# Sparse attention into a Mish MLP on one core: x of batches 4 to 7 transposed by VectorE, strided heads staggered by one block, w_out's second half released by landed v

## The chip, the core and the metric

The kernel runs on one core of a Trainium2 chip. The core has five engines with a queue of instructions each: TensorE (matrix products, PE), VectorE (DVE), ScalarE (ACT), GpSimd (POOL) and SyncE (SP), which here only issues transfers. Each engine works through its own queue in order, and engines wait for one another by semaphores. Data lies in HBM, is moved by DMA into SBUF, and TensorE writes its results to PSUM. The metric is the device time of one execution in microseconds, the median of several runs.

## What is computed

Two layers of work, one behind the other:

```python
# q, k, v: 8 batches x 8 heads x 576 positions x 64
scores = q @ k.T / sqrt(64)
# heads 0 to 3, "local":   0 <= i - j < 32
# heads 4 to 7, "strided": i >= j and i % 32 == j % 32
attn = softmax(where(mask, scores, -1e9)) @ v
x = attn.transpose(0, 2, 1, 3).reshape(4608, 512)
h = x @ w_in                      # 512 -> 2048
g = h * tanh(softplus(h))         # Mish
out = g @ w_out                   # 2048 -> 512
```

## The kernel before

**Blocks.** The MLP works on nine blocks of 512 tokens, t = 0 to 8. In block t the first layer (`mlp1`, L410) makes eight groups of 16 matmuls of 512 columns; a group fills one of three PSUM buffers of two banks (`acc`, L87), which ScalarE empties with Mish. The second layer (`mlp2`, L435) then runs 16 groups of four matmuls into two of these buffers, and ScalarE copies the output out twice per block. The buffers' names rotate from block to block (x, y, z in the loop at L585).

**Attention.** Batch 0 comes ahead of the loop. The attention of batch t + 1 is spread over the second layer of block t: `attn_steps` (L358) gives a list of 16 lists, and the loop at L614 runs list i behind the i-th second-layer group. The steps are Q (`qk`: scores of a part of the units into an `acc` buffer, then ScalarE's exponential into P_s or P_l), M (`mask`, L284: VectorE multiplies by the mask), V (`pv`: four matmuls with v into one of two small PSUM buffers, `tile_t`, then VectorE's reciprocal and product, L311 and L312, into x_s or x_l) and X (`xt`: TensorE transposes x into a `tile_t` buffer and ScalarE copies it to xT, which the first layer of the next block reads). A column of ones beside v gives the sum for the softmax. xT is a ring for four batches. A batch has 16 strided units (in parts of 6, 6 and 4) and 12 local units (5, 5 and 2).

**Inputs.** GpSimd issues the loads of strided q and k, which cast on the way (`load_qk_str`), and of the weights. SP issues the loads of local q and k and of all v as f32 (`load_qk_loc`, `load_v`); GpSimd casts them one block later (`cast_qk_loc`, `cast_v`, L144). From batch 2 on, q and k are turned by transposing transfers on SP (`transpose_by_dma`, L163), put at list 9 of the block before the one that uses them. At the end of block t, SP gets the loads for batch t + 3. SP works in order, so a waiting output or transpose holds back the loads behind it.

**Release of w_out.** The loads of w_in and the first half of w_out are issued ahead of the loop. In `cast_v1` (L574, called in block 0) VectorE casts the strided v of batch 1, and GpSimd then copies four elements of the cast into `held`. That copy only makes GpSimd wait: behind it in its queue stand the loads of w_out's second half, of ks and qs of batch 2, and the casts of batches 1 and 2. In block 0 the second layer goes through w_out a quarter at a time over all four token tiles (`fc_major`), so the third quarter is first needed at its ninth group.

**Order.** All queues are in the order in which the program is written (`manual_schedule`); no scheduler moves anything.

Of the kernel before, what the change touches and what calls it, by code (L numbers as in the profile page):

```python
# [38 lines left out]
def kernel(ctx, tc, q, k, v, moe_w_in, moe_w_out, out):  # L39
# [28 lines left out]
    vs = [const.tile([128, 4, CS, D + 1], BF16, name=f"vs{i}") for i in range(2)]  # L68
    qTl = const.tile([128, 2, S], BF16, name="qTl")
    kTl = const.tile([128, 2, 32 + S], BF16, name="kTl")  # L70
    qTs = const.tile([128, 16 * SU], BF16, name="qTs")
    kTs = const.tile([128, 16 * SU + 48], BF16, name="kTs")
    P_s = [const.tile([PN, 2, n * PN + 56], BF16, name=f"Ps{i}") for i, n in enumerate((6, 6, 4))]
    P_l = [const.tile([128, 2, n * WQ + 32], BF16, name=f"Pl{i}") for i, n in enumerate((5, 5, 2))]
    gate = const.tile([1, 256], BF16, name="gate")
    held = const.tile([1, 4], BF16, name="held")
    x_l = const.tile([128, NW, 256], BF16, name="x_l")
    x_s = const.tile([128, CS, 256], BF16, name="x_s")

    g_pool = ctx.enter_context(tc.tile_pool(name="gp", bufs=2))  # L80
    small = ctx.enter_context(tc.tile_pool(name="small", bufs=4))
# [5 lines left out]
    def acc(i, name):  # L87

        return ps_a.tile([128, 2, 512], F32, tag=f"acc{i}", name=name)

    def tile_t(name):
        return ps_t.tile([128, 512], F32, tag="pt", name=name)


    def load_qk_str(b):
        for dst, src in ((ks, k), (qs, q)):
# [27 lines left out]
    def load_v(b):  # L124
        load_v_str(b)
        load_v_loc(b)
# [33 lines left out]
            "p (t i e d) -> p t i e d", t=2, i=NW, e=2  # L160
        )

    def transpose_by_dma(b):  # L163
        for src, dst in ((ks, kTs), (qs, qTs)):
            nc.sync.dma_start_transpose(
                dst[:, 0:16 * SU].rearrange("c (u n) -> c u n", u=16),
                src[b % 2][0:SU].rearrange("p h x -> p (h x)"),
            )
        for hp in range(2):
            for src, dst in ((kl, kTl[:, hp, 32:32 + S]), (ql, qTl[:, hp, :])):  # L170
                nc.sync.dma_start_transpose(
                    dst.rearrange("c (i n) -> c i n", i=NW),
                    by_tile(src[b % 2])[:, hp].rearrange("p i e d -> p (i e d)"),
                )
# [19 lines left out]
    def t_step(b, kind, which, hp, eng=None):  # L194

        eng = eng or nc.vector
        tr = tile_t("tr")[:].bitcast(BF16)
        if kind == "s":
            src = (qs if which == "q" else ks)[b % 2]
            for u in range(8):  # L200
                h, jj = 2 * hp + u // 4, u % 4
                nc.tensor.transpose(
                    tr[:, PN * u:PN * u + PN],
                    src[0:PN, h, 128 * jj:128 * jj + 128],
                    ident[0:PN, 0:PN],
                )
            dst = (qTs if which == "q" else kTs)[:, 8 * SU * hp:8 * SU * hp + 8 * SU]
# [41 lines left out]
        "s": [S_UNITS[0:6], S_UNITS[6:12], S_UNITS[12:16]],  # L249
        "l": [L_UNITS[0:5], L_UNITS[5:10], L_UNITS[10:12]],  # L250
    }
    AT = {kd: {u: (i, n) for i, p in enumerate(PARTS[kd]) for n, u in enumerate(p)} for kd in "sl"}

    class Attn:
        def __init__(self, b):
# [1 line left out]

        def qk(self, parts, i_acc):

            ps, o = acc(i_acc, "ps"), 0  # L260
            todo = []
            for kind, i in parts:
                w = WQ if kind == "l" else PN
                o0 = o
                for x, y in PARTS[kind][i]:
                    for e in range(2):
                        r = slice(64 * e, 64 * e + 64)
                        if kind == "l":
                            lhsT, rhs = kTl[r, y, WQ * x:WQ * x + 128], qTl[r, y, WQ * x:WQ * x + WQ]
                        else:  # L270
                            c0 = SU * (4 * y + x)
                            lhsT, rhs = kTs[r, c0:c0 + 128], qTs[r, c0:c0 + PN]
                        nc.tensor.matmul(ps[:, e, o:o + w], lhsT=lhsT, rhs=rhs, start=True, stop=True)  # L273
                    o += w
                todo.append((kind, i, o0, o - o0))
            for kind, i, o0, nw in todo:
                n, pt = (128, P_l[i]) if kind == "l" else (PN, P_s[i])
                nc.scalar.activation(pt[0:n, :, 0:nw], ps[0:n, :, o0:o0 + nw], AF.Exp, scale=scale)  # L278

        def mask(self, kind, i, meng):  # L280
            nu = len(PARTS[kind][i])
# [8 lines left out]
        def pv_mm(self, kind, i, po):  # L290
            for h in range(4):
                if kind == "l":
                    n, rhs = 128, vl[self.b % 2][:, i, h, :]
                    part, u = AT["l"][i, h // 2]
                    pt, c0 = P_l[part][:, h % 2], WQ * u
                else:
                    n, rhs = PN, vs[self.b % 2][0:PN, h, i, :]
                    part, u = AT["s"][i // 2, h]
                    pt, c0 = P_s[part][:, i % 2], PN * u
                nc.tensor.matmul(  # L300
                    po[:, h, :], lhsT=pt[0:n, c0:c0 + 128], rhs=rhs,
                    start=True, stop=True,
                )
# [51 lines left out]
                    tr[:, 0:576].rearrange("p (j n) -> p n j", j=CS),  # L355
                )

    def attn_steps(b, x, y):  # L358

        a = Attn(b)  # L360
        Q = lambda i_acc, *parts: (lambda: a.qk(parts, i_acc))
# [4 lines left out]
        if x == y:  # L366
# [13 lines left out]
                [V("l", 3), V("l", 4)],  # L380
                [X("l", 0), X("l", 1)], [],
            ]
        return [
            [],
            [Q(x, s0), Q(y, s1), M(*s0), M(*s1)],
            [],
# [10 lines left out]
            [V("l", 4), X("l", 0)],  # L397
            [X("l", 1)], [],
        ]


    def segs(t):
# [7 lines left out]
    def mlp1(t, accs):  # L410
        gT = g_pool.tile([128, 16, 512], BF16, tag="gT", name="gT")

        held = {}

        def group(g, ccs=(2, 3, 0, 1)):
            if g not in held:
                held[g] = acc(accs[g % 3], "psh")
            ps = held[g]
            for u in range(2):
                fc = 2 * g + u  # L420
                for a, n, o in segs(t):
# [12 lines left out]

    def mlp2(t, gT, accs, fc_major=False):  # L435
        po = {}
# [43 lines left out]
    with tc.manual_schedule():  # L480
# [92 lines left out]

        def cast_v1():  # L574
            cast(Dv, vs[1][0:PN, :, :, 0:D], vs32[0:PN])
            Po.tensor_copy(held[:], vs[1][0:1, 3, 0, 0:4])
            load_w_out(2, 4)
            load_qk_str(2)
            cast_v_loc(1, Po)
            load_v(2)  # L580
            cast_qk_loc(2, Po, Po)
            load_qk_str(3)
            cast_v(2, Po, Po)

        for t in range(NBLK):  # L585
            x, y, z = accs
            if t > 0:
                gT, g1 = mlp1(t, accs)
            ts, at = [], []
# [62 lines left out]
```

## Time and profile before

| what | value |
|---|---|
| median of 4 runs | 325.6 us (324.75 to 328.02) |
| the profiled execution | 326.07 us, its span 324.3 us |
| TensorE matmul busy | 303.4 us (94%) |
| ScalarE busy | 173.5 us (53%) |
| VectorE busy | 105.2 us (32%) |
| GpSimd busy | 90.3 us (28%) |
| first-layer matmuls (L423) | 640, 128.3 us |
| second-layer matmuls (L443) | 512, 127.9 us |
| mean transfer rate | 139 GB/s, 45.15 MB |

Busy time of a matmul overlaps its neighbour's, so the profile's start-to-start distances say more than durations: an undisturbed group of four 512-column matmuls takes 0.86 us. The 40 slices are 8.1 us each. A line of the time line gives the start, the duration, the engine, the line of the code, what is done, how many, and in brackets the engine's idle time before it and what ended it. In the chain of waits each line is a start, a length and what held the end back there. A window's line gives its length, the busy time and instructions of the five engines in turn, the granted TensorE clock, the share of the transfer engines and the rate.

### The profile page before, as it was taken

The numbers are of one execution on the slowest core, as the hardware profiler recorded it, in microseconds if no ns is written. First come the engines' busy times: TensorE is split into PE (matmuls) and PEld (weight loads), VectorE is DVE, ScalarE is ACT, GpSimd is POOL, SyncE is SP. The second block draws the span as 40 slices with busy tenths as digits, with TensorE's granted clock in tenths as the row PEclk, the third lists the DMA queues.
The fourth block names the chain that finished last, engine by engine and source line by source line (L and its number), as shares of the span: only waits on it lengthen the run. The fifth ranks groups of instructions, "written<-read, shape, count | busy, mean of one in ns | idle before, by whom it ended". The sixth has DMA issues, their size and how long they took to land.

```text
span 324.3 us, 5880 instructions
## 1 busy us (share of the span) xinstructions
PE 303.4 (94%) x2488; PEld 160.4 (49%) x2488; DVE 105.2 (32%) x289; ACT 173.5 (53%) x196; POOL 90.3 (28%) x100
## 2 busy tenths in 40 slices
PE   0678996999999998999999999999999999999995
PEld 0563453544455444544568655445544554444444
DVE  8671165510381039202830183018301830000000
ACT  2583652285737572666466745674567457315601
POOL 9288019420273048004700480047000000000000
PEclk9999999799999999999999999999999999999999
DMA  7999999997999996999399939993820101011012
GB/s 185 210 212 205 217 186 221 187 158 190 196 194 150 222 179 139 139 222 166 90 162 190 197 91 167 197 185 94 136 85 0 64 3 67 0 65 65 2 55 74
DMA packets 96985, 45.15 MB, mean 139 GB/s; under 512 B 79040, under 2 KB 89600, under 8 KB 96960
## 3 DMA queue, kind: packets, MB, share of 16 engines
q1 hardware_dynamic: 85520, 35.66, 59.3%
q0 software_dynamic: 11152, 8.92, 18.6%
q8 instruction: 19, 0.31, 0.4%
q10 hardware_dynamic: 288, 0.21, 0.2%
q14 instruction: 6, 0.05, 0.1%
HBM read 36.78 MB, written 9.44 MB: 143 GB/s over the span
## 4 chain that ended last, share of the span: by engine, by line
PE 68%; DVE 12%; DMA 8%; SPq 6%; POOL 2%; ACT 1%; issue 1%; POOLq 0%
PE psh L423 32%; PE pso L443 23%; DMA vl<-in_v_dram 6%; PE pso L470 4%; PE po L300 4%; DMA w_out<-in_moe_w_out_dram 3%; POOL vl L144 2%; SPq L115 2%; DVE x_l L312 2%; SPq L109 2%; PE ps L273 2%; DVE x_s L312 2%; PE trx L339 2%; DVE Pl L284 1%; DVE ks L144 1%
## 5 line engine op out<-in xcount | busy, mean ns | idle before, releaser
L443 PE MATMUL pso<-w_out,gT 128*128 128x512 bf16 x512 | 127.9, 382 | 2.2 <-DMA w_out<-in_moe_w_out_dram 2.2
L423 PE MATMUL psh<-xT,w_in 128*128 128x512 bf16 (+1 forms) x640 | 128.3, 362 | 0.0
L428 ACT ACTIVATE gT<-psh 128x1024 bf16<-128x1024 f32 x72 | 73.6, 1024 | 45.0 <-PE psh L423 44.4
L423 PEld LDWEIGHTS <-w_in 128*128 128x128 bf16 x640 | 63.0, 99 | 62.9 <-issue 2.7
L443 PEld LDWEIGHTS <-gT 128*128 128x128 bf16 x512 | 43.9, 98 | 41.9 <-issue 3.4
L284 DVE TENSOR_TENSOR Ps<-Ps,consts_sb 72x864 bf16<-72x864 bf16 (+1 forms) x24 | 16.9, 706 | 114.9 <-ACT Ps L278 114.9
L142 ACT COPY xT<-trx 128x576 bf16<-128x576 bf16 x32 | 20.1, 638 | 39.6 <-PE trx L349 30.7
L144 POOL CAST kl<-kl 96x768 bf16<-96x768 f32 (+1 forms) x13 | 11.9, 938 | 81.0 <-DMA kl<-in_k_dram 80.9
L144 POOL CAST vl<-vl 128x768 bf16<-128x768 f32 (+2 forms) x30 | 26.0, 867 | 11.7 <-DMA vl<-in_v_dram 9.8
L450 ACT COPY osb<-pso 128x1024 f32<-128x1024 f32 x16 | 16.2, 1012 | 22.6 <-PE pso L443 13.5
L278 ACT ACTIVATE Ps<-ps 72x864 bf16<-72x864 f32 (+1 forms) x24 | 18.5, 804 | 13.3 <-PE ps L273 13.2
L311 DVE RECIPROCAL rden<-po 72x4 f32<-72x4 f32 (+1 forms) x100 | 17.4, 174 | 21.1 <-PE po L300 21.0
L312 DVE TENSOR_TENSOR x_s<-po,rden 72x256 bf16<-72x256 f32 x56 | 23.5, 420 | 1.9
L278 ACT ACTIVATE Pl<-ps 128x960 bf16<-128x960 f32 (+1 forms) x24 | 18.7, 806 | 6.4 <-PE ps L273 5.7
L300 PEld LDWEIGHTS <-Ps 72*128 72x128 bf16 x256 | 14.1, 102 | 14.3 <-DVE Ps L284 2.8
L300 PE MATMUL po<-vs,Ps 72*128 72x65 bf16 x256 | 17.9, 202 | 2.0 <-DVE vs L144 0.9
L312 DVE TENSOR_TENSOR x_l<-po,rden 96x256 bf16<-96x256 f32 x44 | 18.5, 420 | 1.5
L144 DVE COPY osb<-pso 128x512 f32<-128x512 f32 (+1 forms) x2 | 1.1, 558 | 54.5 <-PE pso L470 54.5
L300 PE MATMUL po<-vl,Pl 128*128 128x65 bf16 x192 | 13.1, 202 | 2.6 <-DVE rden L311 1.0
L144 POOL CAST vs<-vs 72x2048 bf16<-72x2048 f32 x6 | 12.0, 2008 | 9.2 <-DMA vs<-in_v_dram 6.1
L144 POOL CAST ql<-ql 96x768 bf16<-96x768 f32 (+1 forms) x13 | 11.9, 939 | 9.2 <-DMA ql<-in_q_dram 9.2
L470 PE MATMUL pso<-w_out,gT 128*128 128x512 bf16 (+1 forms) x80 | 14.0, 336 | 0.0
(65 smaller groups left out, 177.8 us busy)
## 6 DMA issues: line engine op xcount, KB each, us to landing
out_dram<-osb SPq DMA_DIRECT2D x16, 512.0 KB, 4.0
vs<-in_v_dram SPq DMA_DIRECT2D x8, 576.0 KB
vl<-in_v_dram SPq DMA_DIRECT2D x8, 576.0 KB, 9.3
kl<-in_k_dram SPq DMA_DIRECT2D x7, 576.0 KB, 18.0
ql<-in_q_dram SPq DMA_DIRECT2D x7, 576.0 KB, 9.9
w_out<-in_moe_w_out_dram POOLq DMA_DIRECT2D x4, 512.0 KB, 15.2
ks<-in_k_dram POOLq DMA_DIRECT2D x7, 288.0 KB, 8.8
qs<-in_q_dram POOLq DMA_DIRECT2D x7, 288.0 KB, 9.2
```

Source lines behind the costliest of these rows:

```text
L142: nc.scalar.copy(out_, in_)
L144: eng.tensor_copy(out_, in_)
L278: nc.scalar.activation(pt[0:n, :, 0:nw], ps[0:n, :, o0:o0 + nw], AF.Exp, scale=scale)
L284: meng.tensor_tensor(out=pm, in0=pm, in1=mk[0:n, :].unsqueeze(1).unsqueeze(1).to_broadcast([n, 2, nu, w]), op=ALU.mult,)
L300: nc.tensor.matmul(po[:, h, :], lhsT=pt[0:n, c0:c0 + 128], rhs=rhs, start=True, stop=True,)
L311: nc.vector.reciprocal(rden[0:m, :], po[0:m, :, D])
L312: nc.vector.tensor_tensor(out=dst.rearrange("p (h d) -> p h d", h=4), in0=po[0:m, :, 0:D], in1=rden[0:m, :].unsqueeze(2).to_broadcast([m, ...
L423: nc.tensor.matmul(ps[:, u, o:o + n], lhsT=w_in[:, cc, fc * 128:(fc + 1) * 128], rhs=xT[:, cc, a:a + n], start=(cc == 2), stop=(cc == 1),)
L428: nc.scalar.activation(gT[:, 2 * g:2 * g + 2, :], ps[:], AF.Mish)
L443: nc.tensor.matmul(p[:, ot % 2, :], lhsT=gT[:, fc, 128 * ot:128 * ot + 128], rhs=w_out[:, fc, :], start=(fc == 0), stop=(fc == 15),)
L450: nc.scalar.copy(osb[:], p[:])
L470: nc.tensor.matmul(p, lhsT=gT[:, fc, 128 * ot:128 * ot + 128], rhs=w_out[:, fc, c0:c1], start=(fc == 0), stop=(fc == 15),)
```

## The change

Four things are changed together.

1. **x of batches 4 to 7** goes to xT without TensorE. VectorE transposes blocks of 32x32: 12 instructions of 384 elements per partition for the local heads, straight into xT (`xt_loc`), and 12 of 512 for the strided heads into a new buffer xs_t (`xt_str`), which two ScalarE copies bring to xT (`xt_str_copy`). Rows 64 to 95 of x_s are cleared once by GpSimd in block 3, since a transpose reads 96 rows.
2. **The strided heads are staggered by one block from batch 4 on.** Their scores are made one block earlier, in parts of 7, 7 and 2 units (kind "n"), beside the local heads of the batch before; batch 4's at the end of block 2. Their products with v and their transposes run between the first-layer groups of the next block (`str_steps`). The local heads keep their block (`loc_steps`). qTs and kTs are doubled, and loads and transposing transfers of strided q and k move one block ahead: GpSimd issues those of batches 4 and 5 in block 1, and SP issues batch 4's transposes in block 1 between the loads of q, k and of v.
3. **The first layer** of blocks 1 to 8 does the strided half (chunks 2 and 3) of its first three groups before their local half.
4. **`held`** copies from the f32 v, so that GpSimd waits for the transfer and not for VectorE's cast.

```diff
--- before.py
+++ after.py
@@ tiles @@
-    qTs = const.tile([128, 16 * SU], BF16, name="qTs")
-    kTs = const.tile([128, 16 * SU + 48], BF16, name="kTs")
-    P_s = [const.tile([PN, 2, n * PN + 56], BF16, name=f"Ps{i}") for i, n in enumerate((6, 6, 4))]
+    qTs = [const.tile([128, 16 * SU], BF16, name=f"qTs{i}") for i in range(2)]
+    kTs = [const.tile([128, 16 * SU + 48], BF16, name=f"kTs{i}") for i in range(2)]
+    P_s = [const.tile([PN, 2, n * PN + 56], BF16, name=f"Ps{i}") for i, n in enumerate((7, 7, 4))]
+    xs_t = const.tile([128, CS, 2, 96], BF16, name="xs_t")
+    def sT(x, b):
+        return x[(b + 1) % 2 if b else 0]
@@ transposing transfers @@
-    def transpose_by_dma(b):
+    def str_by_dma(b):
         for src, dst in ((ks, kTs), (qs, qTs)):
             nc.sync.dma_start_transpose(
-                dst[:, 0:16 * SU].rearrange("c (u n) -> c u n", u=16),
+                sT(dst, b)[:, 0:16 * SU].rearrange("c (u n) -> c u n", u=16),
                 src[b % 2][0:SU].rearrange("p h x -> p (h x)"),
             )
+
+    def loc_by_dma(b):
         for hp in range(2):
...
@@ parts @@
-    AT = {kd: {u: (i, n) for i, p in enumerate(PARTS[kd]) for n, u in enumerate(p)} for kd in "sl"}
+    PARTS["n"] = [S_UNITS[0:7], S_UNITS[7:14], S_UNITS[14:16]]
+    AT = {kd: {u: (i, n) for i, p in enumerate(PARTS[kd]) for n, u in enumerate(p)} for kd in "sln"}
@@ Attn.qk @@
-            ps, o = acc(i_acc, "ps"), 0
-            todo = []
+            if i_acc is None:
+                ps = [tile_t("ps") for _ in range(2)]
+            else:
+                t = acc(i_acc, "ps")
+                ps = [t[:, 0, :], t[:, 1, :]]
+            o, todo = 0, []
...
-                            lhsT, rhs = kTs[r, c0:c0 + 128], qTs[r, c0:c0 + PN]
+                            lhsT = sT(kTs, self.b + (kind == "n"))[r, c0:c0 + 128]
+                            rhs = sT(qTs, self.b + (kind == "n"))[r, c0:c0 + PN]
...
+                if i_acc is None:
+                    for e in range(2):
+                        nc.scalar.activation(
+                            pt[0:n, e, 0:nw], ps[e][0:n, o0:o0 + nw], AF.Exp, scale=scale
+                        )
+                else:
...
@@ new in Attn @@
+        def xt_loc(self, i0, n):
+            t0 = (self.b % RING) * S
+            src = x_l[:, i0:i0 + n, :].rearrange("p i (c q r) -> p i c q r", c=2, q=4)
+            dst = xT[:, 0:2, t0 + WQ * i0:t0 + WQ * (i0 + n)].rearrange("p c (i m) -> p i c m", i=n)
+            for q in range(4):
+                for m in range(0, WQ, 32):
+                    nc.vector.transpose(
+                        dst[32 * q:32 * q + 32, :, :, m:m + 32], src[m:m + 32, :, :, q, :]
+                    )
+        def xt_str(self):
+            src = x_s[:].rearrange("p j (c q r) -> p j c q r", c=2, q=4)
+            for q in range(4):
+                for m in range(0, 96, 32):
+                    nc.vector.transpose(
+                        xs_t[32 * q:32 * q + 32, :, :, m:m + 32], src[m:m + 32, :, :, q, :]
+                    )
+        def xt_str_copy(self):
+            t0 = (self.b % RING) * S
+            for c in range(2):
+                nc.scalar.copy(
+                    xT[:, 2 + c, t0:t0 + S].rearrange("p (n j) -> p j n", j=CS), xs_t[:, :, c, 0:PN]
+                )
+    def str_steps(b):
+        a = Attn(b)
+        V = lambda i: (lambda: a.pv("s", i))
+        return [
+            [], [], [V(0), V(1)], [V(2), V(3)], [V(4), V(5)], [V(6), V(7), a.xt_str],
+            [], [], [], [], [],
+        ]
+    def loc_steps(b, x, y):
...
+        return [
+            [],
+            [Q(x, ("l", 0)), Q(None, ("l", 2), *n2), Q(y, ("l", 1)), M("l", 0), M("l", 2)],
+            [], [],
+            [V(0), V(1), M("l", 1)],
+            [V(5)] + [Q(x, ("n", 0)), Q(y, ("n", 1))] * more + [a.xt_str_copy],
+            [V(2)],
+            [V(3)],
+            [V(4), lambda: a.xt_loc(0, NW)] + [M("n", 2), M("n", 0), M("n", 1)] * more,
+            [], [], [], [], [], [], [],
+        ]
@@ attn_steps(b, x, y, z=None) @@
+        if z is not None:
+            r[12].append(Q(x, ("n", 0)))
+            r[13].append(Q(z, ("n", 1)))
+            r[15] += [Q(x, ("n", 2)), M("n", 0), M("n", 1), M("n", 2)]
@@ mlp1 @@
-                            rhs=xT[:, cc, a:a + n], start=(cc == 2), stop=(cc == 1),
+                            rhs=xT[:, cc, a:a + n], start=(cc == 2 and o == 0),
+                            stop=(cc == 1 and o + n == 512),
...
-        return gT, [lambda g=g: group(g) for g in range(8)]
+        return gT, [lambda g=g, c=c: group(g, c) for c in ((2, 3), (0, 1)) for g in range(3)] + [
+            lambda g=g: group(g) for g in range(3, 8)
+        ]
@@ the start @@
-        Dv.memset(kTs[:], 0.0)
+        Dv.memset(kTs[0][:], 0.0)
+        Dv.memset(kTs[1][:, 16 * SU:], 0.0)
...
-            Po.tensor_copy(held[:], vs[1][0:1, 3, 0, 0:4])
+            Po.tensor_copy(held[:], vs32[0:1, 3, 0, 0:4])
@@ the loop over t @@
-                at[9].append(lambda: transpose_by_dma(2))
+                at[9] += [lambda: str_by_dma(2), lambda: loc_by_dma(2)]
...
-                if t + 1 < B:
-                    at = attn_steps(t + 1, x, y)
+                if t <= 2:
+                    at = attn_steps(t + 1, x, y, z if t == 2 else None)
+                elif t + 1 < B:
+                    a1 = str_steps(t + 1)
+                    at = loc_steps(t + 1, x, y)
+                if t == 1:
+                    at[9].append(lambda: str_by_dma(3))
+                    at[10].append(lambda: load_qk_str(5))
+                if t == 3:
+                    Po.memset(x_s[64:96], 0.0)
                 if t + 2 < B:
-                    at[9].append(lambda: transpose_by_dma(t + 2))
+                    at[9].append(lambda: loc_by_dma(t + 2))
+                if 1 < t < B - 3:
+                    at[9].append(lambda: str_by_dma(t + 3))
...
+                if i < len(a1):
+                    for s in a1[i]:
+                        s()
...
-            if 0 < t < B - 3:
-                load_qk_str(t + 3)
+            if t == 1:
+                load_qk_str(4)
+            elif 1 < t < B - 4:
+                load_qk_str(t + 4)
...
                 load_qk_loc(t + 3)
+                if t == 1:
+                    str_by_dma(4)
                 load_v(t + 3)
```

More of the change, by code (lines that the diff above doesn't have):

```diff
@@ L206, in t_step @@
                 )
-            dst = (qTs if which == "q" else kTs)[:, 8 * SU * hp:8 * SU * hp + 8 * SU]
+            dst = sT(qTs if which == "q" else kTs, b)[:, 8 * SU * hp:8 * SU * hp + 8 * SU]
             cast(
@@ L271, in qk @@
                             c0 = SU * (4 * y + x)
-                            lhsT, rhs = kTs[r, c0:c0 + 128], qTs[r, c0:c0 + PN]
-                        nc.tensor.matmul(ps[:, e, o:o + w], lhsT=lhsT, rhs=rhs, start=True, stop=True)
+                            lhsT = sT(kTs, self.b + (kind == "n"))[r, c0:c0 + 128]
+                            rhs = sT(qTs, self.b + (kind == "n"))[r, c0:c0 + PN]
+                        nc.tensor.matmul(
+                            ps[e][:, o:o + w], lhsT=lhsT, rhs=rhs, start=True, stop=True
+                        )
                     o += w
@@ L277, in qk @@
                 n, pt = (128, P_l[i]) if kind == "l" else (PN, P_s[i])
-                nc.scalar.activation(pt[0:n, :, 0:nw], ps[0:n, :, o0:o0 + nw], AF.Exp, scale=scale)
+                if i_acc is None:
[4 more added lines that the diff above has]
+                else:
+                    nc.scalar.activation(
+                        pt[0:n, :, 0:nw], t[0:n, :, o0:o0 + nw], AF.Exp, scale=scale
+                    )
         def mask(self, kind, i, meng):
@@ L297, in pv_mm @@
                     n, rhs = PN, vs[self.b % 2][0:PN, h, i, :]
-                    part, u = AT["s"][i // 2, h]
+                    part, u = AT["n" if self.b > 3 else "s"][i // 2, h]
                     pt, c0 = P_s[part][:, i % 2], PN * u
@@ L356, in xt, with attn_steps @@
                 )
-    def attn_steps(b, x, y):
+        def xt_loc(self, i0, n):
[13 more added lines that the diff above has]
+                        xs_t[32 * q:32 * q + 32, :, :, m:m + 32], src[m:m + 32, :, :, q, :]
+                    )
+        def xt_str_copy(self):
[3 more added lines that the diff above has]
+                    xT[:, 2 + c, t0:t0 + S].rearrange("p (n j) -> p j n", j=CS), xs_t[:, :, c, 0:PN]
+                )
+    def str_steps(b):
[6 more added lines that the diff above has]
+    def loc_steps(b, x, y):
+        a = Attn(b)
+        Q = lambda i_acc, *parts: (lambda: a.qk(parts, i_acc))
+        M = lambda kd, i: (lambda: a.mask(kd, i, nc.vector))
+        V = lambda i: (lambda: a.pv("l", i))
+        more = b + 1 < B
+        n2 = (("n", 2),) if more else ()
+        return [
[9 more added lines that the diff above has]
+        ]
+    def attn_steps(b, x, y, z=None):
         a = Attn(b)
@@ L382, in attn_steps @@
             ]
-        return [
+        r = [
             [],
@@ L399, in attn_steps @@
         ]
+        if z is not None:
+            r[12].append(Q(x, ("n", 0)))
+            r[13].append(Q(z, ("n", 1)))
+            r[15] += [Q(x, ("n", 2)), M("n", 0), M("n", 1), M("n", 2)]
+        return r
     def segs(t):
@@ L588 @@
                 gT, g1 = mlp1(t, accs)
-            ts, at = [], []
+            ts, at, a1 = [], [], []
             if t == 0:
```

## The prediction

> **What bounds the kernel now.** I read the page's busy table and slices first, then the chain that ended last, then the time line and the windows of the places where that chain leaves TensorE.
>
> ```profile
> PE   0678996999999998999999999999999999999995
> DVE  8671165510381039202830183018301830000000
> PEclk9999999799999999999999999999999999999999
> DMA  7999999997999996999399939993820101011012
> PE 68%; DVE 12%; DMA 8%; SPq 6%; POOL 2%; ACT 1%; issue 1%; POOLq 0%
> ```
>
> TensorE is full from slice 3 on. Slice 6 is the one deep hole, and the granted clock drops in slice 7, just behind it. VectorE is empty for most of each block and nearly full for one slice in four. The transfers are full until about 154 us and then have one free slice per block (3). The chain of waits around slice 6:
>
> ```profile
> 46.05 1.14 DVE vs L144
> 47.25 0.18 POOL held L576
> 47.48 9.05 DMA w_out<-in_moe_w_out_dram
> 56.58 1.02 PE pso L443 x4
> 58.04 1.82 PE pso L443 x4
> 60.30 1.46 PE pso L443 x4
> 58.00:59.00 1.00, 1.00 (x6) 0.41 (x4) 0.96 (x2) 0.92 (x1) 0.89 (x2) 0.50 1.24 189
> ```
>
> GpSimd issues the second half of w_out only after VectorE's cast of v. It lands at 56.5, when TensorE has waited 2.2 us, and the next matmuls run at half clock (0.50 in the window's third column from the end): four take 1.82 us instead of the 0.86 of every undisturbed group. The windows show 0.50 from 58 to 61 and 0.81 in the next one, some 3.4 us, so 1.7 us lost. The hole costs 2.2 + 1.7 = 3.9 us.
>
> Later blocks, by the chain's first-layer starts, last 34.08 (t=2), 32.83, 33.02, 32.48, 32.48 (t=6) and, without attention, 27.63 us (t=7). The attention's own matmul time follows from start-to-start distances in the time line: scores 0.50 + 0.53 + 0.32 = 1.35; fourteen products with v at 0.13 = 1.8; four groups of x transposes at 0.26 = 1.04. With 27.63 that is 31.8; the blocks hold 0.7 to 1.2 us of waits on top, and t=2 holds 2.3. In t=2:
>
> ```profile
> 122.09 1.90 POOL L144 CAST vs<-vs 72x2048 bf16<-72x2048 f32 x1 [1.32 <-DMA vs<-in_v_dram]
> 122.21 2.08 DVE L284 TENSOR_TENSOR Ps<-Ps,consts_sb 72x576 bf16<-72x576 bf16 x1
> 126.45 0.29 PE L300 MATMUL po<-vl,Pl 128*128 128x65 bf16 x4 [0.99 <-DVE rden L311]
> ```
>
> A mask that takes 0.45 us alone took 2.08 beside a GpSimd cast, and TensorE stood for 1.3 us behind it.
>
> **What the Trainium skill says.** "SBUF — State Buffer", section "Who interferes with whom": a VectorE instruction with two SBUF inputs contends with GpSimd reads for whole instructions, one with a single input outside the two-port modes does not. The trace agrees on the mask (0.45 to 2.08); on a transpose no run shows it yet. "VectorE: DVE Perf Modes", section "The three transpose paths", gives 311 ns for 128x128 in 32x32 blocks; its section "Two Vector instructions with no wait between them" says that an instruction which starts in another quadrant than the one before waits until that has finished. "TensorE: Matmul & The Clock Gate", section "HAM oscillation — how this bites in real kernels": an idle wait makes the clock gate fall back; the trace agrees at 58 us, though its wait was 2.2 us and the page speaks of 3.4.
>
> **The change part by part.**
>
> *w_out's release.* The held copy reads v's f32 buffer when it has landed, not VectorE's cast. The load of v was issued at 34.68 and GpSimd is idle from 32.5 to 47.25. Landing isn't shown. The SP queue gives a sign: the issue of the k load behind it ends at 43.5 after 7.7 us of back-pressure, so I take 43 (bounds 39 and 45.9, when the cast ran unwaited). GpSimd is free about 4.3 us earlier, and everything queued behind it (w_out, ks and qs of batch 2, the casts, the v load that SP holds for them, and by ks's landing the transposes and the outputs) moves as much. The third quarter would land at 52 and is due at 54.2; the hole closes. Next is the last quarter: TensorE took it up at 63.3 without a wait, so it had landed by then; 4.3 earlier is 59.0 at the latest, and it will be due at 63.3 - 3.9 = 59.4. **-3.9** (bounds -4.5 and 0, if full transfers only reorder).
>
> *Start.* Larger Ps memsets and the second kTs add about 0.25 us on VectorE before its first cast; that cast waits for data and beside GpSimd's memsets anyway: 0.
>
> *x of batches 4 to 7.* 28 TensorE transposes go per batch: -1.04 us in each of t=3 to 6, and the two waits beside them (158.94 to 159.28, 162.66 to 162.94). ScalarE's four copies of 0.64 become two, off the path. VectorE gets 24 transposes per batch. Price: 311 ns less 128 elements at one per cycle (133) is 178 fixed; an instruction of 384 elements comes to 0.58 us (estimate), of 512 to 0.71. Local: 12 x 0.58 = 6.9 us (bounds 6.0 if each starts 0.08 before the last ends, as a reciprocal does behind a product, 8.2 if the quadrant change adds 0.1 each); strided 8.5. The strided ones run in the first layer, where VectorE is idle today, and end about 15 us into the block, before the masks at 18: hidden. The local ones start 1.0 us after the last product with v. Behind them in VectorE's queue stand three masks for the next batch, and the first strided products wait for the second of these: 1.0 + 6.9 + 0.3 + 0.7 = 8.9 us. TensorE gets there after seven second-layer groups (6.05) and three half groups of the first layer (2.6), 8.8 us. So it is even: 0 to 1.3 us of wait, I take 0.4. The local transposes alone (7.9) are in time for the half groups that read them.
>
> *Half groups.* The first layer now starts three groups on the strided half. That wants the third PSUM buffer 1.7 us into the block; the output copy that frees it ended 1.1 us in (134.98 + 1.01). ScalarE's first activation comes 0.9 later and its buffer is wanted 1.7 later than before: 0.
>
> *Stagger.* Products with v, two at a time in the first layer with two PSUM buffers, against 0.6 us of VectorE each: 0.35 us of wait per block. Scores cost 1.45 instead of 1.35. A block is then 27.63 + 1.45 + 1.8 + 0.35 + 0.4 = 31.65. t=4: 31.8 with the 0.17 of its half-width matmuls, -1.2. t=5: -0.85. t=6 has no scores for a next batch (-0.67): 31.0, -1.5. Sum **-3.55**. t=7, t=8: 0.
>
> *t=2* takes batch 4's strided scores: +0.67. Their last exponential stands behind the output copy on ScalarE (0.3 + 1.0 + 0.3), and the second half group of t=3 wants that PSUM buffer after 1.0: +0.6. Block times shift against the GpSimd casts, so of the 1.3 us mask stall I take 0.8 off. **+0.5** (bounds -0.5, +1.5).
>
> *t=3 and the queues.* In t=1 GpSimd now also issues ks and qs of batch 5, behind the transposes of batch 3 that free the buffers; next on GpSimd are the k casts, idle until 115 anyway. SP puts the k and q transposes of batch 4, which wait for ks (issued 98.4, 8.8 to land), ahead of the v loads. Two loads of 0.58 MB and two transposes of 0.33 MB are 1.8 MB, some 10 us at the 178 GB/s of that stretch; transfers had only 2 to 3 us free there (0.18 at 122 to 124). v of batch 4 landed at 122 and 124.3 before; less the 4 gained, plus 10 less 2, that is 128 and 130. GpSimd then casts (1.9, then 3.8), issues two loads (1.4) and clears x_s (1.8, as its 16x2048 memset took): 137.2. VectorE's first write of x_s waits for that. t=3 starts at 134.9 - 3.9 + 0.5 = 131.5, TensorE stops at the third product, 3.7 us in, 135.2, until 137.7: +2.5 (bounds 0 and 5), and half a chance of the 1.7 of a fallen clock, +0.9. Behind that write stand the other strided products and their transposes, which have VectorE's free time until 18 us. The block: 31.65 - 0.4 + 3.4 = 34.65, **+1.8**. Moved transposes of batches 5 to 7 replace others in SP's queue one for one: 0.
>
> Sum: -3.9 - 3.55 + 0.5 + 1.8 = -5.15 on the profiled 326.07 (span 324.3 and 1.8 around it): 320.9. It ran 0.5 above the median, so against 325.6 I predict **320.4**.
>
> **The rivals.** (1) *VectorE becomes the bound, slower.* No VectorE transpose is in the trace. Each 0.1 us above 0.58 delays the masks by 1.2 us in each of t=4 to 6, and above 0.64 the first layer of t=4 to 7 too. At 0.72 us the gain is gone; at 0.8 the time is about 330, at 1.0 about 340. For it: two-byte elements in small strided blocks, a new quadrant every time. Against: the page's price. (2) *The release does nothing*: v lands late, or w_out lands no sooner because transfers are full: 3.9 back, 324.3. For it: DMA at 9 in slices 1 to 8. Against: nine microseconds from issue to landing at 47.5, in the same crowd. (3) *No wait for the clearing of x_s*: back-pressure hides the added transfers, v comes in time: 3.4 better, 317. (4) *A longer one*: v five us later, with the clock: 325 to 326.
>
> **How the numbers follow.** One per cent is 3.3 us, about what can be told from no change here. Chances: forecast 0.46 (318 to 323), (1) 0.13, (2) or (4) 0.22, (3) 0.19. Faster by over 1% (below 322.3): most of the forecast's, all of (3), a little of (2): 0.66. Within: 0.21. Slower (above 328.9): 0.13, nearly all of (1). The range runs from (3) with a small extra to just past (4): 316 to 327.
>
> **What would show it.** Right: no wait for w_out near 54 us and no clock of 0.5 behind it; VectorE transposes of 0.55 to 0.65 us; blocks t=4 to 6 of 31 to 32 us; a VectorE wait on GpSimd's memset in t=3 with a TensorE gap of some 2 us. Wrong: transposes over 0.7 us, TensorE waiting at the first strided products of t=4 to 6, or a hole that only moves to w_out's last quarter, due at about 59.

## The result, and the profile after

Over 11 runs the changed kernel takes 327.3 us in the median (324.6 to 329.46); over 16 runs beside them the kernel before takes 327.39 (320.75 to 331.3). The ratio is 1.0137, with a 95% interval of 1.0071 to 1.0202. Ratios, here and below, count of each kernel only the runs within 1.5% of its shortest, and of the kernel before, whose runs spread over 10 us, that leaves out the larger part; so the medians agree and the ratio doesn't. The gain of 5 us that was forecast did not come. The profiled execution took 327.27 us, its span is 325.5 us (before 324.3), and the mean granted clock is 0.988.

The busy slices of the page of the changed kernel, for the engines whose lines were shown of before:

```profile
PE   0778999999999999659999999999999999999995
DVE  8671167600750076139689958994899590000000
PEclk9999999999999999969999999999999999999999
DMA  6999999999999999999929992799160011011012
```

Counted from 0, the hole of slice 6 is gone and a new one stands in slices 16 and 17, and the clock drops in the second of them. The transfers, which had room in slice 15 and a gap in slice 19 before, are full through slice 19. The blocks, from one first-layer start to the next in the time lines of the two profiled executions, say which stretches gained and which lost:

| block | before, us | after, us | difference | predicted |
|---|---|---|---|---|
| t=0 | 41.62 | 38.12 | -3.5 | -3.9 |
| t=1 | 32.55 | 32.72 | +0.2 | 0 |
| t=2 | 34.09 | 34.35 | +0.3 | +0.5 |
| t=3 | 32.83 | 40.28 | **+7.5** | +1.8 |
| t=4 | 33.02 | 31.91 | -1.1 | -1.2 |
| t=5 | 32.48 | 31.81 | -0.7 | -0.85 |
| t=6 | 32.48 | 31.07 | -1.4 | -1.5 |
| t=7 | 27.62 | 27.63 | 0 | 0 |

One block is off. The time line of its place, GpSimd first and then TensorE (start, length, engine, line, operation, output<-input, and in brackets the idle time before and what ended it):

```profile
131.65 1.89 POOL L149 CAST vs<-vs 72x2048 bf16<-72x2048 f32 x1 [5.45 <-PE pso L530]
134.49 3.28 POOL L149 CAST vl<-vl 128x768 bf16<-128x768 f32 x4 [0.94 <-DMA vl<-in_v_dram]
137.72 0.72 POOL L102 DMA_DIRECT2D ks<-in_k_dram  x1
138.42 0.70 POOL L102 DMA_DIRECT2D qs<-in_q_dram  x1
139.17 1.80 POOL L693 MEMSET x_s<- 32x2048 bf16 x1
...
141.00 0.42 DVE L335 TENSOR_TENSOR x_s<-po,rden 72x256 bf16<-72x256 f32 x1 [5.80 <-POOL x_s L693]
141.47 0.94 PE L323 MATMUL po<-vs,Ps 72*128 72x65 bf16 x8 [5.51 <-DVE x_s L335]
```

This is to be read upwards. TensorE stands 5.51 us for VectorE's write of x_s; VectorE waits for the clearing; the clearing stands in GpSimd's queue behind two loads of strided k and q, and behind the casts of v of batch 4, of which the local half landed at about 134.5. Before, the same cast started 10.2 us sooner:

```profile
124.28 3.73 POOL L144 CAST vl<-vl 128x768 bf16<-128x768 f32 x4 [0.29 <-DMA vl<-in_v_dram]
```

The windows of four microseconds around the wait in the changed kernel (span, busy time and count of TensorE, its weight loads, VectorE, ScalarE and GpSimd; then granted clock, share of the DMA engines, GB/s; the share adds up the time of all packets, so it can pass 1):

```profile
136.00:140.00 4.00, 0.00 (x0) 0.00 (x0) 0.00 (x0) 1.02 (x1) 3.85 (x5) 1.00 0.82 130
140.00:144.00 4.00, 2.38 (x14) 1.13 (x15) 1.99 (x7) 0.00 (x0) 0.96 (x1) 0.55 1.26 146
144.00:148.00 4.00, 4.00 (x27) 2.06 (x26) 2.48 (x9) 2.05 (x2) 0.00 (x0) 0.60 1.30 108
```

The clock falls to 0.55 and 0.60 behind the gap. From 141.47 to 148 that costs about 6.5 x 0.42 = 2.7 us; with the wait of 5.5 it is 8.2, and an undisturbed block of t=3, measured below, is 31.95 long, 8.3 shorter than this one.

### The profile page after: what moved, and what is told of

The parts are those of the page before. It is cut to its first block, busy times and chain, and to the rows that moved or that the text cites. A ratio compares the mean times of both kernels' runs of the same rounds, so it can differ in the third digit from the quotient of the medians.

```text
span 325.5 us, 5770 instructions
## 1 busy us (share of the span) xinstructions
PE 300.4 (92%) x2376; PEld 157.7 (48%) x2376; DVE 165.2 (51%) x386; ACT 183.2 (56%) x195; POOL 87.9 (27%) x101
## 4 chain that ended last, share of the span: by engine, by line
PE 69%; DVE 15%; DMA 10%; POOL 3%; issue 1%; ACT 1%; SPq 0%; POOLq 0%
PE psh L507 33%; PE pso L530 23%; DVE xT L388 6%; DMA ql<-in_q_dram 4%; PE pso L557 4%; PE po L323 4%; DMA lq<-in_k_dram 3%; DMA vl<-in_v_dram 2%; DVE x_s L335 2%; PE ps L286 2%; DVE Ps L307 2%; DVE x_l L335 1%; DVE rden L334 1%; POOL vl L149 1%; DVE Pl L307 1%
## 5 line engine op out<-in xcount | busy, mean ns | idle before, releaser
L507 PE MATMUL psh<-xT,w_in 128*128 128x512 bf16 (+1 forms) x640 | 133.5, 366 | 0.3 <-ACT Ps L299 0.3
L530 PE MATMUL pso<-w_out,gT 128*128 128x512 bf16 x512 | 121.8, 379 | 0.0
L307 DVE TENSOR_TENSOR Ps<-Ps,consts_sb 72x864 bf16<-72x864 bf16 (+3 forms) x24 | 13.7, 591 | 41.5 <-ACT Ps L299 41.4
L397 DVE STREAM_TRANSPOSE xs_t<-x_s 32x512 bf16<-32x512 bf16 x48 | 33.7, 702 | 0.9
L388 DVE STREAM_TRANSPOSE xT<-x_l 32x384 bf16<-32x384 bf16 x48 | 27.3, 569 | 0.7
L149 POOL CAST vl<-vl 128x768 bf16<-128x768 f32 (+2 forms) x30 | 23.1, 769 | 6.5 <-DMA vl<-in_v_dram 5.1
L299 ACT ACTIVATE Ps<-ps 72x864 bf16<-72x864 f32 (+3 forms) x21 | 17.4, 861 | 12.8 <-PE ps L286 12.7
L404 ACT COPY xT<-xs_t 128x576 bf16<-128x576 bf16 x8 | 21.4, 2933 | 0.0
L307 DVE TENSOR_TENSOR Pl<-Pl,consts_sb 128x960 bf16<-128x960 bf16 (+1 forms) x24 | 15.1, 642 | 10.6 <-ACT Pl L299 10.6
L147 ACT COPY xT<-trx 128x576 bf16<-128x576 bf16 x16 | 9.9, 637 | 14.7 <-PE trx L372 11.5
```

The source lines that it names most:

```text
L149: eng.tensor_copy(out_, in_)
L299: nc.scalar.activation(pt[0:n, :, 0:nw], t[0:n, :, o0:o0 + nw], AF.Exp, scale=scale)
L307: meng.tensor_tensor(out=pm, in0=pm, in1=mk[0:n, :].unsqueeze(1).unsqueeze(1).to_broadcast([n, 2, nu, w]), op=ALU.mult,)
L388: nc.vector.transpose(dst[32 * q:32 * q + 32, :, :, m:m + 32], src[m:m + 32, :, :, q, :])
L397: nc.vector.transpose(xs_t[32 * q:32 * q + 32, :, :, m:m + 32], src[m:m + 32, :, :, q, :])
L404: nc.scalar.copy(xT[:, 2 + c, t0:t0 + S].rearrange("p (n j) -> p j n", j=CS), xs_t[:, :, c, 0:PN])
```

## The experiments

All times are medians; the kernel before ran beside them on the same chip. There it took 326.25 us over 71 runs (320.26 to 331.24) in the first set (E1 to E4), 326.07 over 21 (319.35 to 332.08) in the second (E5 to E8). Ratios are to it. My theory after the result: the wait for the clearing of x_s, with the clock behind it, is the whole loss. The rival: transposing by VectorE or the stagger lengthens that block anyway.

**E1: clearing ahead of the loop.** The rows 64 to 95 of x_s are cleared once before the loop, where the other memsets stand.

```diff
             Po.memset(x[0][64:SU], 0.0)
+        Po.memset(x_s[64:96], 0.0)
         load_qk_loc(2)
...
-                if t == 3:
-                    Po.memset(x_s[64:96], 0.0)
```

> The clearing of x_s stands ahead of the loop instead of behind block 2's casts. Theory A (the late clearing is what ate the gain): the 5.5 us wait of VectorE on GpSimd and the half clock behind it go, block 3 falls from 40.3 us to about 32, and the time to about 319.5, 2.4% below the changed kernel. Rival B (VectorE's transposes, or v landing late, hold block 3 as well): the wait moves to the next thing, block 3 stays above 37 us and the time above 324.

Measured: 320.09 us (317.33 to 322.61), ratio 0.9934 [0.9886, 0.9982], span 319.4. The block of t=3 is 31.95, so all of its loss belonged to the wait and what followed, and the rival falls. The time line of TensorE shows a wait in another place, and the windows behind it:

```profile
117.28 0.43 PE L286 MATMUL ps<-qTl,kTl 64*128 64x96 bf16 x12 [1.75 <-DMA qTl<-ql]
137.90 0.30 PE L323 MATMUL po<-vs,Ps 72*128 72x65 bf16 x4 [0.17 <-DVE x_s L335]
```

```profile
114.00:118.00 4.00, 2.25 (x41) 1.34 (x41) 1.66 (x6) 0.51 (x2) 0.00 (x0) 1.00 1.17 213
118.00:122.00 4.00, 4.00 (x20) 1.61 (x18) 2.94 (x9) 1.41 (x3) 0.06 (x1) 0.61 1.35 189
```

At 137.90, where the changed kernel stood 5.51, it is 0.17. But in t=2 the transposed q of batch 3 came 1.75 us late, with a clock of 0.61 behind it, and that block is 37.28 instead of 34.35. This run took 321.22 us; in 15 of the 20 runs the mean clock was 0.998 or more, so most of them hardly had that lowered clock. The DMA engines, not only the clearing, are close to the path.

**E2: the release of w_out taken back**, all else as changed.

```diff
-            Po.tensor_copy(held[:], vs32[0:1, 3, 0, 0:4])
+            Po.tensor_copy(held[:], vs[1][0:1, 3, 0, 0:4])
```

> The changed kernel with held copied from VectorE's cast again, the rest as changed. Theory A (releasing w_out early holds back k, q and v of batches 2 to 4, which makes the clearing late): the hole for w_out near 54 us and the half clock come back, +3.5 us in block 0, but v of batch 4 lands some 2 to 3 us earlier and block 3 starts 3.5 later, so the wait for the clearing falls from 5.5 us to about 0 and the clock stays; the time is 322 to 325. Rival B (the release has nothing to do with the clearing): v of batch 4 lands 3.5 us later, the wait stays at 5.5 and the time is about 331.

Measured: 325.75 us (322.5 to 328.98), ratio 1.0038 [0.9997, 1.0078], span 325.4, as long as with the release. The first wait is back and the second has shrunk:

```profile
58.26 1.44 PE L530 MATMUL pso<-w_out,gT 128*128 128x512 bf16 x4 [3.48 <-DMA w_out<-in_moe_w_out_dram]
...
134.71 3.68 POOL L149 CAST vl<-vl 128x768 bf16<-128x768 f32 x4 [0.93 <-DMA vl<-in_v_dram]
142.10 0.29 PE L323 MATMUL po<-vs,Ps 72*128 72x65 bf16 x4 [1.44 <-DVE x_s L335]
```

Block t=0 is 5.3 us longer than in the changed kernel, block t=3 4.8 shorter (35.47). The local cast of v starts at 134.71, with the release at 134.49: the release does not bring v of batch 4 forward. TensorE only arrives sooner at the same late clearing, and the gain of t=0 is given back there.

**E3: the release alone**, in the kernel before: the same line with vs32.

> The kernel before with the release of w_out alone. Theory A: the hole of 2.2 us and the half clock go, block 0 is 3.5 us shorter, everything else as before: 1.1% faster, with no wait for later transfers. Rival B (the transfers that w_out overtakes come late and cost TensorE as much): block 1 or 2 is longer by 2 us or more, and the time within 0.3% of before.

Measured: 321.28 us (320.2 to 322.74), ratio 0.9947 [0.9918, 0.9976], span 319.9, clock 1.0. The median is 5.0 us under that of before, the ratio only 0.5%: the gain depends on which runs of before it is held against (E9). Where nothing late stands behind it, the release keeps its gain: the first block is 37.41 and no window from 48 to 64 us has a clock under 1.00. Again v of batch 4 did not come sooner; its local cast, at 124.28 before:

```profile
126.13 3.29 POOL L144 CAST vl<-vl 128x768 bf16<-128x768 f32 x4 [0.67 <-DMA vl<-in_v_dram]
```

**E4: early clearing, late release**, E1 and E2 together: the changes from t=3 on by themselves.

> The clearing ahead of the loop and held from VectorE's cast. Theory A: as the first run of this group, plus the hole in block 0: about 323, 3.5 us above it. Rival B (late transfers matter elsewhere in the first of them): equal to it or below.

Measured: 322.48 us (320.24 to 326.42), ratio 0.9982 [0.9942, 1.0022], span 320.7. Blocks t=3 to t=6 are 31.94, 31.92, 32.25 and 31.07, against 32.83, 33.02, 32.48 and 32.48 before: 3.6 us less. For these four the sum had 5.1: 3.55 for t=4 to t=6, which gain 2.7 here, and 1.6 for t=3 without its wait (31.65 less 0.4, against 32.83), which gains 0.9. The spread of before hides this in the ratio, and the profiled run of before was the shortest here: these four blocks take 130.8, 132.2 and 132.8 us in the three profiles with the attention of before (before, E3, E9), and 127.1 to 127.9 in the four with the early clearing (E1, E4, E5, E7). So the saving is there, by 2.9 to 5.7 us.

**Why v of batch 4 comes so late.** SP issued its strided half at 110.11 before and at 124.96 in the changed kernel, behind the load of q, whose issue took 7.22 us, and the two transposes, 5.23 and 2.14. Two parts of the change put work ahead of it in t=1 and t=2: on SP the transposes of batch 4's strided k and q (E6 takes them back behind v), and on GpSimd the loads of batch 5's (E8 moves them to t=2; E7 is E8 with E1's clearing).

```diff
-                if t == 1:
-                    str_by_dma(4)
                 load_v(t + 3)
+                if t == 1:
+                    str_by_dma(4)
```

> The changed kernel, with the two transposed loads of batch 4's strided q and k issued behind the loads of its v in stage 1, not ahead of them; the clearing stays where the change has it. In the changed kernel the two transposes hold SP's queue from 117.4 to 124.9, v is issued at 125.0 and the cast of it starts at 131.7. Theory A (v is late because SP issues it behind these transposes): v is issued near 117.5, its casts start near 124.5, the clearing ends by 135, and the wait of 5.5 us in front of the strided attention of stage 3 is gone, with the half clock behind it: the block of t=3 falls from 40.3 to about 32.5. The transposed q of batch 4 then lands some 2.1 us later, and the wait for it in t=2, 0.66 us before, grows to about 2.7; time about 321. Rival B (the DMA engines are full, and the order of issue on SP is not what sets the landing): v's casts start at 130 or later, the wait stays at 4 us or more, time 325 or more.

Measured: 329.8 us (329.1 to 330.13), ratio 1.0166 [1.0088, 1.0244], span 328.3. The casts come at 130 or later, as rival B has it; the wait for the clearing is gone all the same, but for another reason than theory A's.

```profile
118.73 3.22 SPq L120 DMA_DIRECT2D vs<-in_v_dram  x1
122.06 0.47 SPq L124 DMA_DIRECT2D vl<-in_v_dram  x1
...
130.31 1.89 POOL L149 CAST vs<-vs 72x2048 bf16<-72x2048 f32 x1 [2.47 <-DMA vs<-in_v_dram]
132.57 3.28 POOL L149 CAST vl<-vl 128x768 bf16<-128x768 f32 x4 [0.37 <-DMA vl<-in_v_dram]
135.67 0.60 PE L286 MATMUL ps<-qTs,kTs 64*128 64x72 bf16 x14 [6.58 <-DMA qTs<-qs]
```

v's two loads were issued 6.2 and 4.3 us sooner (124.96 and 126.35 in the changed kernel), and their casts start 1.3 and 1.9 sooner; the transposed q of batch 4 lands 8.3 later (127.38), and TensorE stands 6.58 us for it, so that it comes to the clearing long after that is done. The block of t=3 is 32.01, that of t=2 46.69, 12.3 longer: this wait, one of 1.77 us for the local q of batch 3, and half clock behind both. Another order only chose another transfer to be late.

```diff
-                    at[10].append(lambda: load_qk_str(5))
...
                 cast_qk_loc(t + 2, Po, Po)
+                if t == 2:
+                    load_qk_str(5)
                 cast_v(t + 2, Po, Po)
```

> The changed kernel, with the loads of batch 5's strided k and q issued by GpSimd in stage 2 between the casts of batch 4's q and k and those of its v, no longer in stage 1; the clearing stays where the change has it. They are 0.58 MB, about 3 us of what the DMA engines move there (about 190 GB/s). Theory A (these bytes stand ahead of batch 4's q and v): the 7.2 us in which SP issues the load of q falls to about 4, all behind it on SP moves 3 us up, v's casts start near 128.7, and the wait for the clearing falls from 5.5 to about 2.6 us; time about 323. Rival B (the bytes delay v just as much from their new place, or the transposes alone set it): casts start at 131 or later, wait 5 us or more, time about 326 or 327.

Measured: 326.44 us (323.38 to 328.03), ratio 1.0143 [1.0098, 1.0188], span 326.3. Rival B, nearly: SP issues q in 5.41 us instead of 7.22 and v 1.9 us sooner, and v's strided half gains 2.7, but the local half, now beside the moved loads, loses 1.8. From the time line:

```profile
128.97 2.37 POOL L149 CAST vs<-vs 72x2048 bf16<-72x2048 f32 x1 [4.38 <-PE ps L286]
136.28 3.28 POOL L149 CAST vl<-vl 128x768 bf16<-128x768 f32 x4 [4.94 <-DMA vl<-in_v_dram]
143.26 0.95 PE L323 MATMUL po<-vs,Ps 72*128 72x65 bf16 x8 [7.86 <-DVE x_s L335]
```

The wait for the clearing grows to 7.86. But landings vary from one execution to the next: E7, with the same transfers in the same order, has these two casts at 126.31 and 130.29. What speaks against theory A is the time of all 18 runs, then, and not this one profile. That the engines are full is seen in the windows of 16 us, the kernel before first and then the changed one (last two columns: share of the DMA engines, GB/s):

```profile
112.00:128.00 16.00, 14.73 (x148) 7.08 (x145) 8.61 (x23) 9.00 (x11) 9.01 (x10) 1.00 0.92 162
128.00:144.00 16.00, 15.89 (x114) 7.96 (x113) 3.78 (x12) 9.38 (x11) 1.38 (x3) 1.00 1.21 179
144.00:160.00 16.00, 15.81 (x149) 7.73 (x148) 6.91 (x21) 10.38 (x12) 9.63 (x11) 1.00 0.72 116
```

```profile
112.00:128.00 16.00, 15.23 (x189) 8.17 (x188) 10.17 (x32) 8.53 (x12) 3.19 (x4) 1.00 1.20 179
128.00:144.00 16.00, 10.09 (x84) 4.83 (x83) 4.79 (x13) 6.64 (x8) 8.14 (x8) 0.89 1.16 179
144.00:160.00 16.00, 16.00 (x107) 7.66 (x106) 11.60 (x22) 10.42 (x14) 3.12 (x4) 0.90 1.25 194
```

In these 48 us 552 against 457 GB/s, times 16 us, are 1.5 MB more. Only part of this is what the stagger brings forward: from the start to 112 us the mean is 188 GB/s, and 196 before, so 0.9 MB are catching up; to 160 us it is 187, and 183 before, so 0.6 MB are ahead. Before, two of the three windows had room; after, none has.

> The kernel with the clearing ahead of the loop (320.1 us before this), with the loads of batch 5's strided k and q moved from stage 1 to stage 2 in addition. Theory A: the transposed q of batch 3 lands some 3 us earlier, so its wait of 1.75 us in stage 2 goes, and with it the half clock behind it: the block of t=2 falls from 37.3 to about 32.7, all others stay, time about 315.5. Rival B (the bytes come back where q, k and v of batches 4 and 5 land): the block of t=2 falls but that of t=3 or t=4 grows by 2 us or more, time 318 to 320.

Measured: 318.27 us (317.96 to 320.17), ratio 0.9826 [0.9745, 0.9906], four runs, span 316.2, clock 1.0, and the lowest median of all kernels tried: 9 us under that of the changed kernel. Nothing on the path waits for v's casts any more. The wait for the transposed q is gone, no slice has a lowered clock, and the blocks from t=2 on are 33.63, 31.94, 32.26, 31.80, 31.08 and 27.63; t=2 fell by 3.65 from E1's 37.28. Whether the move of the loads did this is open: E1's own runs reach 317.33, most of them at full clock, and its profiled run was one of those that were not.

The forecast for this run was 315.5, with a block of 32.7 for t=2: that left out the scores of batch 4 that the change moves into t=2 (E3, which lacks them, has 32.59 there), and it took the whole wait off E1's median, though the profiled run that had the wait was 1.1 us above it.

**E5: ScalarE's copy of the strided x**, with E1's clearing. In the changed kernel it reads densely and writes 2 bytes every 16; here it writes densely and reads 2 bytes every 384.

```diff
-  xT[:, 2 + c, t0:t0 + S].rearrange("p (n j) -> p j n", j=CS), xs_t[:, :, c, 0:PN]
+  xT[:, 2 + c, t0:t0 + S].rearrange("p (n j) -> p n j", j=CS),
+  xs_t[:, :, c, 0:PN].rearrange("p j n -> p n j"),
```

> The kernel with the clearing ahead of the loop, with ScalarE's two copies of the strided part of x written in the order of the destination: dense writes, strided reads. Theory A (the 2.93 us of such a copy come from writing 2 bytes every 16, and they lie beside other work): a copy takes 1 us or less, and the time does not move, 320 within 1.5 us. Rival B (ScalarE's 5.9 us in stages 4 to 6 delay the outputs' copies or the exponentials on the path): the blocks of t=4 to t=6 fall by 0.5 us or more each, time about 318. Rival C (reading with the stride costs as much as writing with it): a copy stays above 2 us, time unchanged.

Measured: 321.23 us (318.49 to 326.09), ratio 0.9876 [0.9735, 1.0017], span 318.6. The groups by line, of E1 and then of E5:

```profile
L404 ACT COPY xT<-xs_t 128x576 bf16<-128x576 bf16 x8 | 21.4, 2931 | 0.0
```

```profile
L404 ACT COPY xT<-xs_t 128x576 bf16<-128x576 bf16 x8 | 9.2, 1204 | 0.0
```

A copy falls from 2.93 to 1.20 us, which lies between what A and C expected, and the blocks of t=5 and t=6 stay (31.81, 31.07); t=4 is 33.09, not shorter than E1's 32.55. So ScalarE's 1.7 us per copy lay beside other work.

**E9: the kernel before, profiled again**, because its runs spread over 10 us.

> The kernel before, unchanged, looked at again: its runs lie between 319 and 332 us, and in the quickest of them the granted clock is 1.0, while it is 0.993 to 0.995 in those near 326. Theory A: the hole at w_out's second half, with its half clock, is not there in every run; a profile of a quick one shows no wait for w_out above 0.5 us in stage 0, full clock from 48 to 64 us, a first block of about 37.5 us in place of 41.6, and a span near 319. Then the part of the change that releases w_out earlier makes certain what some runs of before have by luck. Rival B: the hole is in every run, and the quick ones are quick for another reason (a later wait that is not there): the first block stays at 41 us or more.

Measured: 325.96 us (319.99 to 332.09); the profiled execution was one of 332.09, so a short one was not seen, and A and B stay undecided for it. It showed the opposite end:

```profile
58.55 1.87 PE L443 MATMUL pso<-w_out,gT 128*128 128x512 bf16 x4 [4.32 <-DMA w_out<-in_moe_w_out_dram]
```

The hole at w_out is 4.32 us here and 2.2 in the first profile, and the first block 44.29 against 41.62. Its length varies by itself from one execution to the next. In the runs of this set the clock is 0.998 to 1.0 in all eight below 323.5 us, but also in two of 324.41 and 325.17, and E3, without the hole, has 320.2 to 322.74. That the short runs of before are those without the hole fits this, but is argued, not shown. If it is so, the 3.9 us of the release could be gained only on the longer runs, and the profiled run of before was one of these; against the shorter ones E3 gains 0.5%, some 1.7 us.

## Why the prediction was wrong

The prediction said 320.4 us. The profiled execution is 327.27 against the sum's 320.9; the table above puts 5.6 of these 6.4 us in t=3.

**The step that failed** is the one on t=3: "v of batch 4 landed at 122 and 124.3 before; less the 4 gained, plus 10 less 2, that is 128 and 130". The casts that wait for it started at 131.65 and 134.49.

"Less the 4 gained" rested on the sentence that everything queued behind the release "moves as much", and this is false: E2 without the release has 131.88 and 134.71, and E3, the release alone, has v 1.5 and 1.9 us later than before. GpSimd did issue 3.4 us sooner, but the transfers as a whole got no further: up to 80 us the mean is 186 GB/s in the changed kernel, 188 in E3 and 196 before. The bound for this, "0, if full transfers only reorder", was written beside the hole at w_out and not carried to v.

"Plus 10" was right and "less 2" was not: 131.65 and 134.49 are 9.6 and 10.2 later than before's 122.09 and 124.28. By the start of the local cast some 25.6 MB had been moved, 23.7 before (190 and 191 GB/s from the start): 1.8 MB more, as the prediction had counted. So the free time of before took up none of the added bytes. That bytes set the landing is how these figures read; E6 and E8 only changed their order, and no run took them away.

The sum itself has a slip as well. 122 and 124.3, less 4 and plus 8, are 126 and 128.3; 128 and 130 come out only if the "less 2" is left away. By luck the slip made up for one of the two errors, so that the figures put down were 3.7 and 4.5 us too early and not 5.7 and 6.2.

The clearing then ended at 140.97 instead of 137.2, and TensorE stood 5.5 us instead of 2.5. **The clock** was the second part: half a chance of 1.7 us was taken, and it fell and cost about 2.7. The block's base was 0.7 longer: 31.95 without the wait (E1), where 31.65 less 0.4 was taken. This is rival (4), priced at 325 to 326 and put down together with (2) at 0.22.

**What held.** The release: the held copy ran at 43.81 (43 was taken), no wait for w_out and no lowered clock in t=0, -3.5 against -3.9. The fear that the hole moves to the last quarter did not come true. In the groups by line of the changed kernel:

```profile
L397 DVE STREAM_TRANSPOSE xs_t<-x_s 32x512 bf16<-32x512 bf16 x48 | 33.7, 702 | 0.9
L388 DVE STREAM_TRANSPOSE xT<-x_l 32x384 bf16<-32x384 bf16 x48 | 27.3, 569 | 0.7
```

The local ones (L388) take 0.57 us and the strided ones 0.70, estimated at 0.58 and 0.71 from the Trainium skill, "VectorE: DVE Perf Modes", section "The three transpose paths", so the page's price for 128x128 carries over to these sizes, and rival (1), the only slower one, falls. Those that ran beside a GpSimd cast took no longer (at most 0.57 and 0.71 us), which the prediction had left open. Twelve local ones take 6.97 us (6.9) and the strided ones 8.57 (8.5). Blocks t=4 to t=6 gained 3.2 of the 3.55 in the changed kernel and 2.7 in E4. The waits in front of products with v there are 0.25 and 0.15 us, for the small PSUM buffers, where 0.35 was taken; the 0.4 for the masks does not show.

**What was mis-sized without effect.** ScalarE's two copies got no price of their own beside the 0.64 of the copies from PSUM and took 2.93; "off the path" held (E5). In t=2 the transposed q of batch 4 came 0.66 us late, which the sum did not have; against it, the mask did not stall at all (0.44 us in place of 2.08), where 0.8 of 1.3 was taken off, and the 0.6 for a PSUM buffer is 0.26 and falls in t=3. The 1.82 us for four matmuls at half clock is a duration, to be held against 1.02 and not against the 0.86 from start to start; the 1.7 us lost came from the windows and does not rest on it.

## What to carry to other kernels

Where the DMA engines are full, a transfer that is asked for earlier makes another one later: count bytes up to the stage that needs them, not places in a queue, and don't let a gain at the head of the queue travel down to every transfer behind it. An instruction that needs no data, such as a clearing, must not stand in a queue behind casts that wait for transfers if the path waits for it: moving one memset was worth 6 to 7 us here. And a gain ahead of a late arrival is no gain until that arrival is off the path: by the medians the same release brought 5 us alone, 2.4 with the clearing early (E4 to E1), and nothing in front of the late clearing.

## What the runs showed that was not expected

- The Trainium skill, "TensorE: Matmul & The Clock Gate", section "HAM oscillation — how this bites in real kernels", warns of idle gaps of TensorE above about 3.4 us. Here the clock falls behind shorter waits: to 0.57 behind 1.44 us (E2, t=3), 0.57 behind 2.03 (E4), 0.61 behind 1.75 (E1), as means of four-microsecond windows. It isn't certain at the short end: behind 1.45 us in E5 it stayed at 1.00. The mean clock is 0.86 over 140 to 152 us in E2, and 0.88 over 54 to 68 in E4 and over 112 to 126 in E1: about 1.7 us lost each, so by this estimate a single wait of 1.5 to 2 us can cost about twice itself.
- ScalarE's copy of 128x576 from SBUF to SBUF took 2.93 us when it wrote 2 bytes every 16 and read densely, and 1.20 when it read 2 bytes every 384 and wrote densely. The Trainium skill, "SBUF — State Buffer", section "Door 1: The DMA port swizzle (why `[64,N]` ≈ `[32,N]`)", says that each step to a new line of 16 bytes costs. Both copies step to a new line with every element, one in writing and the other in reading; that the write pays so much more the page doesn't say.
